# Groups of 8, 8, 8, 4, 4, 4 tiles in the routing of a retention + expert + SoLU kernel, parts of its first loads, and the order of two short stretches

## The chip, the cores and the metric

One Trainium2 chip, of which the kernel uses one core. The metric is device time in microseconds (us) of one execution. Engines by their short names: PE (TensorE, matmuls), DVE (VectorE), ACT (ScalarE), POOL (GpSimd), SP (SyncE, which issues most DMAs).

## What is computed

Three blocks in a row, on 8 batches of 576 positions (4608 tokens, 512 features), all in float32:

```python
# 1: retention attention, 8 heads of 64
scores = (q @ k.T) / 8
ret = scores * where(i >= j, gamma[h] ** (i - j), 0)   # a decay, no softmax
x = ret @ v                                            # heads side by side: 4608 x 512
# 2: one expert of eight for each token
expert_idx = argmax(x @ w_gate); gate_w = softmax(x @ w_gate)[expert_idx]
out[mask_e] = gate_w * (relu(x[mask_e] @ w1[e]) @ w2[e])
# 3: SoLU feed-forward
h = out @ w_in                       # 512 -> 1024
solu = h * softmax(h); ln = (solu - mean) / sqrt(var + 1e-6) * g_ln
return ln @ w_out                    # 1024 -> 512
```

## The kernel before, in words

Each engine runs its instructions in the order in which the program writes them; there is no scheduler behind it.

**Stage 1, attention and routing (0 to about 166 us).** 40 chunks, n = 0 to 39: five for each batch, four of 128 positions and one of 64. `load(n)` brings keys, queries, scaled keys and values (`kc`, 1 MB; rows Q, KT, KR, VR), from SP, seven chunks ahead; chunks 0 and 1 come in two halves, and behind the first half of chunk 0 stand the tables `kt_t` (key decay) and `dt_t` (decay between positions, 640 KB). `prep(n)` scales K and Q on POOL (`kc`, `qp`). `scores(n)` (L445) makes `ps` on PE and multiplies it by the decay on DVE (`pp`, L448); `ps` has two buffers, which one chunk fills, so the scores of one chunk wait for the `pp` of the one before. `chunk(n)` adds the state's part (L466: `po` from `qp` and the state `st`) and the chunk's own (L474), then updates the state's sums (L483, `pu`) and copies them to `st` on DVE. `scores(n + 1)` is written ahead of `chunk(n)`. Each 128 finished tokens go through `xtile` (L517: transposed, with the gate's logits beside it, `px`), and when a group of tiles is full, `route(g)` begins.

`route` is a generator: one-hots of the top expert (`oha`), ranks on PE (`pr`, L581 to L585), the gate weight, the scaled tokens `xo` (written to DRAM as `xd`), the index lists by two one-hot tables (`m`, L189 to L195) and a product on PE (`inverse`, `pm`, L203). `tick(budget)` takes steps of it after each chunk; a `yield "pe"` holds it until the next chunk. Groups up to the last but two hold twice ahead of the ranks and twice ahead of `inverse`. With group EARLY (3) the first expert is settled: `count` (L241), its list, and the gathers of its tokens on POOL (L368).

**Stage 2, experts (to about 633 us).** For each expert 8 hidden blocks twice (`ph`, L854: three products of split halves), `hh` and `hl` on ACT and DVE, then outputs (`py`, L869), copied by ACT to `yo` (two buffers) and written to `yd` by SP (L977, L979). Weights come by `raw` (L170) and are split in `wh` (ACT) and `wl` (DVE, L179). `plan` works beside the first expert, by steps written between the blocks (`step`): it finds where each token of the sorted list goes. It writes the lists to DRAM (`sd`, L287) and gathers 36 columns from there (`got`, L318, POOL).

**Stage 3, feed-forward (to the end).** Tiles are taken in pairs q. `prod(q, i)` makes pieces of the first matmul (hx, hy, hz, L1059); `b11`, `b12`, `b21`, `b22` sum two pieces into a tile `wof` and take its maximum on DVE (L1072); `smax` (L1088, L1091), `ssum`, `root`, `norm` make the softmax and the normalisation; `ltrans` transposes the tile on PE (`ptl`, L1142) and splits it; `proj` is the last matmul (`pf`, L1157); `split` halves the inputs of a later pair. For q = 0 the order is written out apart. A tile's `wof` has two buffers.

Of the kernel before, what the change touches and what calls it, by code (L numbers as in the profile page):

```python
# [9 lines left out]
F32 = mybir.dt.float32  # L10
# [26 lines left out]
GROUPS = [8, 8, 8, 6, 3, 3]  # L37
# [85 lines left out]
def kernel(ctx: ExitStack, tc, kvc, kq4, v4, wg, w12, win, wout, gln,  # L123
# [8 lines left out]
    sd = tc.dram_tile([P * NCOL, 1], I32, name="sd")  # L132
# [111 lines left out]
    def plan(pool, col, then):  # L244
# [42 lines left out]
        nc.sync.dma_start(sd.rearrange("(p c) o -> p (c o)", p=P), src)  # L287
        then(numi)
        yield
# [13 lines left out]
        V.tensor_tensor(out=ge, in0=ge, in1=bc(gap, 1, NTT), op=ALU.mult)  # L303
        yield
        V.tensor_reduce(out=off, in_=ge, axis=AX.X, op=ALU.add)
        yield
        ii = T("ii", 2, NTT, dt=I32)
        V.tensor_tensor(out=off, in0=off, in1=C("slot"), op=ALU.add)
        V.tensor_scalar(out=ii[:, 0], in0=off, scalar1=float(NCOL * P - 1), scalar2=None, op0=ALU.min)
        yield  # L310
        V.tensor_scalar(out=ii[:, 1], in0=ii[:, 0], scalar1=7, scalar2=None, op0=ALU.logical_shift_right)
        V.tensor_scalar(out=ii[:, 0], in0=ii[:, 0], scalar1=P - 1, scalar2=None, op0=ALU.bitwise_and)
        yield
        V.scalar_tensor_tensor(out=ii[:, 0], in0=ii[:, 0], scalar=float(NCOL), in1=ii[:, 1], op0=ALU.mult, op1=ALU.add)
        yield
# [28 lines left out]
        V.scalar_tensor_tensor(out=ii[:, 0], in0=tt[:, 1], scalar=2.0 ** 20, in1=tt[:, 0], op0=ALU.mult, op1=ALU.add)  # L344
        yield
        V.tensor_scalar(out=smod, in0=ii[:, 0], scalar1=P - 1, scalar2=None, op0=ALU.bitwise_and)
        V.tensor_scalar(out=sdiv, in0=ii[:, 0], scalar1=7, scalar2=None, op0=ALU.logical_shift_right)
        V.tensor_tensor(out=dst, in0=got, in1=big, op=ALU.add)
# [24 lines left out]
    with ExitStack() as ax:  # L373
# [21 lines left out]
        def load(n):  # L395
# [60 lines left out]
        def chunk(n, ready):  # L456
# [4 lines left out]
            old, new = st[(c + 1) % 2], st[c % 2]  # L461
            po = ps_o.tile([P, 2, NP, P], F32, name="po")[:, :, :2]
            if c > 0:
                for pr in range(NP):
                    for h2, r in enumerate(HALF):
                        nc.tensor.matmul(po[HALF[h2 ^ pr % 2], pr % 2, pr // 2, :cl], old[r, pr, :], qp[r, pr, :cl],  # L466
                                         start=(pr < 2), stop=False, skip_group_check=True)
            for pr in range(NP):
                for to, r_ in enumerate(HALF):
                    h2 = to ^ pr % 2  # L470
                    h, r = 2 * pr + h2, HALF[h2]
                    a, w = (kc[:, VR, h * D:h * D + D], pp[:, h2, pr, :]) if c < 4 else \
                        (kc[r, VR, pr * D:pr * D + D], pp[r, 0, pr, :cl])
# [887 lines left out]
```

## Time and profile before

| | us |
|---|---|
| three runs | 1055.81, 1056.70, 1058.21 (median 1056.7) |
| the profiled execution | 1054.61 |
| its span, first to last instruction | 1052.8 |
| PE busy in it | 1010.9 (96%) |
| DVE, ACT, POOL busy | 652.1, 450.4, 269.2 |
| mean granted clock of PE | 0.986 of 2.4 GHz |

The rows below are of that one execution. In a row of the timeline stand start, duration, engine, line, operation, the tiles written and read, their shape, a count (`x16`: sixteen alike in a run), and in brackets how long the engine was idle ahead of it and what ended the idle time. PEld is PE's weight load. A row SPq is SP's queue of issues; DMA transfers are named by the tile that they fill.

### The profile page before, as it was taken

The numbers are of one execution on the slowest core, as the hardware profiler recorded it, in microseconds if no ns is written. First come the engines' busy times: TensorE is split into PE (matmuls) and PEld (weight loads), VectorE is DVE, ScalarE is ACT, GpSimd is POOL, SyncE is SP. The second block draws the span as 40 slices with busy tenths as digits, with TensorE's granted clock in tenths as the row PEclk, the third lists the DMA queues.
The fourth block names the chain that finished last, engine by engine and source line by source line (L and its number), as shares of the span: only waits on it lengthen the run. The fifth ranks groups of instructions, "written<-read, shape, count | busy, mean of one in ns | idle before, by whom it ended". The sixth has DMA issues, their size and how long they took to land.

```text
span 1052.8 us, 20697 instructions
## 1 busy us (share of the span) xinstructions
PE 1010.9 (96%) x8108; PEld 918.7 (87%) x8108; DVE 652.1 (62%) x1646; ACT 450.4 (43%) x847; POOL 269.2 (26%) x290
## 2 busy tenths in 40 slices
PE   5999996999999999999999999799999999999997
PEld 5888885899999999999999998588888888888885
DVE  3466786543447787789963426666657666666652
ACT  1344344333333344444333426455554555545542
POOL 3626421177310202010100021232232232322211
PEclk9999997999999999999999999899999999999999
DMA  9877973255243534354542231111111111111001
GB/s 333 332 245 298 339 252 133 82 165 167 79 162 114 193 124 167 128 188 153 169 141 102 103 106 39 50 42 49 41 50 50 52 51 40 51 41 41 24 28 42
DMA packets 52614, 130.77 MB, mean 124 GB/s; under 512 B 7680, under 2 KB 22272, under 8 KB 48672
## 3 DMA queue, kind: packets, MB, share of 16 engines
q1 hardware_dynamic: 45312, 109.94, 30.3%
q0 software_dynamic: 7200, 19.46, 5.7%
q8 instruction: 66, 1.08, 0.4%
q14 instruction: 36, 0.29, 0.1%
HBM read 99.95 MB, written 29.42 MB: 123 GB/s over the span
## 4 chain that ended last, share of the span: by engine, by line
PE 76%; DVE 1%; issue 1%; ACT 1%; DMA 1%; POOLq 0%; POOL 0%; ACTq 0%
PE py L869 20%; PE ph L854 20%; PE pf L1157 17%; PE hx L1059 7%; PE hz L1059 4%; PE hy L1059 4%; PE ptl L1142 3%; PE px L837 1%; DMA x<-xd,src 0%; DVE wof L1099 0%; ACT raw L1102 0%; ACT wh L1144 0%; DMA out_dram<-o__11972,dst 0%; DMA out_dram<-o__12074,dst 0%; ACT raw L1091 0%
## 5 line engine op out<-in xcount | busy, mean ns | idle before, releaser
L869 PE MATMUL py<-hh,wh 128*128 128x344 f32 (+7 forms) x512 | 157.6, 308 | 0.0
L869 PE MATMUL py<-hl,wh 128*128 128x344 f32 (+7 forms) x512 | 154.7, 302 | 0.0
L869 PE MATMUL py<-hh,wl 128*128 128x344 f32 (+7 forms) x512 | 154.5, 302 | 0.0
L368 POOL DMA_INDIRECT x<-xd,src x42 | 42.5, 1012 | 284.2 <-PE px L837 222.8
L856 ACT ACTIVATE hh<-ph 128x344 fp32r<-128x344 f32 (+7 forms) x128 | 53.6, 424 | 109.1 <-PE ph L854 105.5
L179 DVE TENSOR_TENSOR wl<-raw,wh 128x1024 fp32r<-128x1024 f32 x64 | 78.5, 1227 | 33.0 <-ACT wh L178 32.8
L869 PEld LDWEIGHTS py<-hh,wh 128*128 128x128 f32 x512 | 96.4, 188 | 0.1
L869 PEld LDWEIGHTS py<-hh,wl 128*128 128x128 f32 x512 | 96.5, 188 | 0.0
L869 PEld LDWEIGHTS py<-hl,wh 128*128 128x128 f32 x512 | 96.2, 188 | 0.0
L854 PE MATMUL ph<-xh,wh 128*128 128x344 f32 (+7 forms) x512 | 94.0, 306 | 1.1 <-ACT xh L840 1.1
L854 PE MATMUL ph<-xl,wh 128*128 128x344 f32 (+7 forms) x512 | 94.0, 306 | 0.0
L854 PE MATMUL ph<-xh,wl 128*128 128x344 f32 (+7 forms) x512 | 94.0, 306 | 0.0
L857 DVE SCALAR_TENSOR_TENSOR hl<-ph,hh 128x344 fp32r<-128x344 f32 (+7 forms) x128 | 60.1, 471 | 52.2 <-ACT hh L856 52.1
L871 ACT COPY yo<-py 128x344 f32<-128x344 f32 (+7 forms) x64 | 26.5, 413 | 141.8 <-PE py L869 111.8
L1157 PE MATMUL pf<-wol,wh 128*128 128x512 f32 x288 | 80.5, 402 | 0.0
L854 PEld LDWEIGHTS ph<-xh,wh 128*128 128x128 f32 x512 | 79.0, 191 | 1.3 <-ACT xh L840 1.3
L854 PEld LDWEIGHTS ph<-xl,wh 128*128 128x128 f32 x512 | 79.0, 190 | 0.2 <-DVE xl L841 0.2
L854 PEld LDWEIGHTS ph<-xh,wl 128*128 128x128 f32 x512 | 79.0, 190 | 0.0
L1145 DVE TENSOR_TENSOR wl<-ptl,wh 128x512 fp32r<-128x512 f32 x72 | 49.5, 689 | 47.6 <-ACT wh L1144 47.6
L1157 PE MATMUL pf<-woh,wh 128*128 128x512 f32 x288 | 76.4, 406 | 1.5 <-ACT wh L1144 1.5
L1157 PE MATMUL pf<-woh,wl 128*128 128x512 f32 x288 | 71.8, 391 | 0.0
L178 ACT CAST wh<-raw 128x1024 fp32r<-128x1024 f32 x64 | 67.0, 1047 | 0.0
(605 smaller groups left out, 2120.5 us busy)
## 6 DMA issues: line engine op xcount, KB each, us to landing
raw<-in_w_dram SPq DMA_DIRECT2D x64, 512.0 KB, 3.5
kc<-in_kvc_dram SPq DMA_DIRECT2D x30, 1024.0 KB, 7.7
yg<-yd SPq DMA_DIRECT2D x72, 128.0 KB, 2.2
xd<-xo SPq DMA_DIRECT2D x3, 2048.0 KB, 8.8
f<-in_win_dram SPq DMA_DIRECT2D x16, 256.0 KB, 3.8
f<-in_wout_dram SPq DMA_DIRECT2D x16, 256.0 KB, 3.7
kc<-in_kvc_dram SPq DMA_DIRECT2D x4, 512.0 KB, 8.4
kc<-in_kq_dram SPq DMA_DIRECT2D x8, 256.0 KB, 7.7
```

The source lines that it names most:

```text
L178: nc.scalar.copy(wh, raw)
L179: V.tensor_tensor(out=wl, in0=raw, in1=wh.bitcast(F32), op=ALU.subtract)
L368: nc.gpsimd.indirect_dma_start(out=x[:w, i, :], out_offset=None, in_=xd[:rows, :], in_offset=bass.IndirectOffsetOnAxis(ap=src[:w, e * CT + ...
L854: nc.tensor.matmul(ph, w[:, w0 + kb * P:w0 + kb * P + P], xx[:, kb, cc], start=(n == 0), stop=(n == 3 * KD - 1))
L856: nc.scalar.activation(out=hh[:, cc], in_=ph, func=AF.Relu)
L857: V.scalar_tensor_tensor(out=hl[:, cc], in0=ph, scalar=0.0, in1=hh[:, cc].bitcast(F32), op0=ALU.max, op1=ALU.subtract)
L869: nc.tensor.matmul(p, w[:, ff], h[:, cc], start=(n == 0), stop=(n == 3 * NFB - 1))
L871: nc.scalar.copy(yo[:, cc], p)
L1059: nc.tensor.matmul(p, x[:, 2 * a + k], m[:, w, k], start=(first and k == 0 and i == 0), stop=(k == 1 and i == 2), skip_group_check=True)
L1142: nc.tensor.transpose(p[:, kb, :], u[:, f * P:f * P + P], ident)
L1145: V.tensor_tensor(out=ll[:, fs, :], in0=p, in1=lh[:, fs, :].bitcast(F32), op=ALU.subtract)
L1157: nc.tensor.matmul(pfs[t], a[:, f, :], w[f // 2][:, f % 2, :], start=(n == 0), stop=(n == m - 1))
```

## The change

It does four things.

At the start, the decay table comes as its first 1024 columns (512 KB) and, after chunk 3, the last 256. The second half of chunk 0 comes as values and then scaled keys, 256 KB each. The products of chunk 1 with the state and its state products are written ahead of the scores of chunk 2.

Groups are 8, 8, 8, 4, 4, 4 and not 8, 8, 8, 6, 3, 3; group 3 holds once and not twice; `tick` has larger budgets from chunk 31 on.

`plan` makes the lists on PE: it transposes the list table (48 x 128), writes eight lists of 6 x 128 one after the other at register offsets into one row in DRAM, reads that row back as 36 x 128 and transposes it again. The gathers go, and so do the index operations for them.

In the third stage, for q = 0, `b11(2)`, `ltrans(1, 1)`, `ltrans(2, 0)` and `prod(2, 3)` change places.

```diff
-GROUPS = [8, 8, 8, 6, 3, 3]
+GROUPS = [8, 8, 8, 4, 4, 4]
...
-    sd = tc.dram_tile([P * NCOL, 1], I32, name="sd")
+    sd = tc.dram_tile([1, NT + CT * P], F32, name="sd")
...
-        nc.sync.dma_start(sd.rearrange("(p c) o -> p (c o)", p=P), src)
         then(numi)
+        sf = T("sf", NCOL)
+        V.tensor_copy(sf[:, :CT], src[:, :CT])
+        V.tensor_copy(sf[:, CT:], f.rearrange("p i c -> p (i c)"))
+        row = pool.tile([NTT, P], F32, name="row")
+        V.memset(row, 0.0)
+        nc.sync.dma_start(sd[0, :NT].rearrange("(t p) -> t p", p=P), row)
+        for _ in range(5):
+            yield
+        pt = psum.tile([NCOL, P], F32, name="pst", tag="pr")
+        nc.tensor.transpose(pt, sf, ident)
+        lists = pool.tile([NCOL, P], F32, name="lists")
+        V.tensor_copy(lists, pt)
...
-        got = T("got", NTT, dt=I32)
-        for t in range(NTT):
-            nc.gpsimd.indirect_dma_start(
-                out=got[:, t:t + 1], out_offset=None, in_=sd[:, :],
-                in_offset=bass.IndirectOffsetOnAxis(ap=ii[:, 0, t:t + 1], axis=0))
+        for e in range(E):
+            nc.sync.dma_start(sd[0, bass.ds(at[e], CT * P)].rearrange("(c p) -> c p", p=P), lists[e * CT:(e + 1) * CT])
             yield
...
+        nc.sync.dma_start(row, sd[0, :NT].rearrange("(t p) -> t p", p=P))
...
+        pd = psum.tile([P, NTT], F32, name="psd", tag="pr")
+        nc.tensor.transpose(pd, row, ident[:NTT, :NTT])
+        V.tensor_tensor(out=dst, in0=pd, in1=big, op=ALU.add)
...
                 if n == 0:
+                    nc.sync.dma_start(dt_t[:, :H * P], dtab[:, :H * P])
+                    nc.sync.dma_start(kc[:, VR], kvc[b, c, :, VR * DM:(VR + 1) * DM])
                     nc.sync.dma_start(kt_t, ktab)
-                    nc.sync.dma_start(dt_t, dtab)
-                nc.sync.dma_start(kc[:, 2:], kvc[b, c, :, 2 * DM:].rearrange("p (a f) -> p a f", a=2))
+                    nc.sync.dma_start(kc[:, KR], kvc[b, c, :, KR * DM:(KR + 1) * DM])
+                else:
+                    nc.sync.dma_start(kc[:, 2:], kvc[b, c, :, 2 * DM:].rearrange("p (a f) -> p a f", a=2))
...
+            if n == 1:
+                upd()
+                scores(n + 1)
+                prep(n + 2)
...
-            tick(1.0)
+            tick(1.0 if n < NN - 9 else 1.5)
...
-            if g < len(GROUPS) - 2:
+            if g < EARLY:
                 yield "pe"
...
         qdma(2 * P, S - P)
+        nc.sync.dma_start(dt_t[:, H * P:], dtab[:, H * P:])
...
-            if n > 0:
+            if n > 1:
                 scores(n + 1)
...
-            tick(0.8 if n < NN - 3 else 2.0)
+            tick(0.8 if n < NN - 9 else 1.5 if n < NN - 3 else 2.0)
...
                     ssum(t + 2)
-                    b11(q + 2)
                     smax(t + 3)
...
                     prod(q + 2, 2)
+                    ltrans(t + 1, 1)
+                    b11(q + 2)
                     root(t + 3)
-                    ltrans(t + 1, 1)
+                    prod(q + 2, 3)
+                    split(q + 3, 1)
                     norm(t + 3)
-                    ltrans(t + 2, 0)
-                    split(q + 3, 1)
...
                 proj(t + 1, 0)
+                if q == 0:
+                    ltrans(t + 2, 0)
...
-                prod(q + 2, 3, 4)
+                prod(q + 2, *((3, 4) if q else (4,)))
```

`upd` is the state update that stood at the end of `chunk` before (the products into `pu` and the copy to `st`). The memset of `wgi` goes ahead of the first `prep`, and the cast of `tri` from chunk 0 to chunk 2.

The start on PE, before: the first rows of its program, from the scores of chunk 0 on (`x16` covers the scores of chunks 1 and 2).

```order
L445 MATMUL ps<-kc 128x128 x8
L474 MATMUL po<-pp,kc 64x128 x8
L483 MATMUL pu<-kc 64x64 x8
L445 MATMUL ps<-kc 128x128 x16
L466 MATMUL po<-qp,st_126 64x128 x8
L474 MATMUL po<-pp,kc 64x128 x8
L483 MATMUL pu<-kc 64x64 x8
L517 MATMUL px<-wgi,xts 64x136 x8
```

And with the change (L448 is `scores` now, L481 the state's part, L493 the chunk's own, L472 the state products):

```order
L448 MATMUL ps<-kc 128x128 x8
L493 MATMUL po<-pp,kc 64x128 x8
L472 MATMUL pu<-kc 64x64 x8
L448 MATMUL ps<-kc 128x128 x8
L481 MATMUL po<-qp,st_126 64x128 x8
L472 MATMUL pu<-kc 64x64 x8
L448 MATMUL ps<-kc 128x128 x8
L493 MATMUL po<-pp,kc 64x128 x8
L528 MATMUL px<-wgi,xts 64x136 x8
```

The scores of chunk 2 stood right behind those of chunk 1; now two pieces of chunk 1 stand between them.

The last chunks on DVE, before, from the decay products of chunk 38 (`pp`, L448) to those of chunk 39 (L450): the scaling and the index chain of group 3, of which three operations follow later.

```order
L448 TENSOR_TENSOR pp<-ps,dt_t 128x512 x2
L485 COPY st_126<-pu 128x256
L567 TENSOR_SCALAR xo<-xr,gt 128x512 x3
L598 TENSOR_SCALAR far<-rka 128x6
L599 SCALAR_TENSOR_TENSOR tm<-tm,rka 128x6
L602 SCALAR_TENSOR_TENSOR sl<-far,tm 128x6
L604 TENSOR_SCALAR smod<-sl 128x6
L605 TENSOR_SCALAR sdiv<-sl 128x6
L189 TENSOR_TENSOR m_2466<-cs,smod 128x768
L450 TENSOR_TENSOR pp<-ps,dt_t 128x4x64
```

With the change the same chain stands between the products of chunks 36 and 37 (`pp`, L451):

```order
L451 TENSOR_TENSOR pp<-ps,dt_t 128x512 x2
L474 COPY st_126<-pu 128x256
L578 TENSOR_SCALAR xo<-xr,gt 128x512 x2
...
L616 TENSOR_SCALAR sdiv<-sl 128x4
L189 TENSOR_TENSOR m_2345<-cs,smod 128x512
L192 TENSOR_TENSOR m_2346<-cs,sdiv 128x4x48
L194 TENSOR_SCALAR m_2346<-m_2346,cs 128x4x48
L195 TENSOR_TENSOR m_2346<-m_2346,cs 128x4x48
L179 TENSOR_TENSOR wl<-raw,wh 128x1024
L451 TENSOR_TENSOR pp<-ps,dt_t 128x512 x2
```

It is complete now ahead of the next products, and a weight split (`wl`) stands behind it.

The third stage on DVE, q = 0, before, from the first of `ssum` (L1104) to the second tile's sum (L1099):

```order
L1104 TENSOR_SCALAR rs__8333<-s__8236 128x1
L1105 RECIPROCAL rs__8333<-rs__8333 128x1
L1107 SCALAR_TENSOR_TENSOR r_8336<-rs__8333 128x1
L1072 ISA wof,hm<-hy,xs_8264 128x512
L1072 ISA hm 128x1
L1088 TENSOR_SCALAR nm<-hm 128x1
L1114 TENSOR_SCALAR v<-v,r_8336 128x1
L1099 ISA wof,nu<-raw,wof 128x1024
```

And with the change (L1085 would be `b11`, L1101 the negated maximum, L1112 the sum):

```order
L1117 TENSOR_SCALAR rs__8309<-s__8212 128x1
L1118 RECIPROCAL rs__8309<-rs__8309 128x1
L1120 SCALAR_TENSOR_TENSOR r_8312<-rs__8309 128x1
L1101 TENSOR_SCALAR nm<-hm 128x1
L1127 TENSOR_SCALAR v<-v,r_8312 128x1
L1112 ISA wof,nu<-raw,wof 128x1024
```

The two rows of `b11` are gone from here; they stand 12 rows further down, behind the splits of the transposed tile (`wl`).

## Rows read from the trace of the kernel before

**Rows 1.** Busy time by stretch: busy us and instructions of each engine, clock, DMA share, GB/s.

```profile
0.00:26.30 26.30, 15.54 (x220) 13.97 (x222) 8.75 (x18) 3.81 (x6) 9.02 (x13) 0.94 0.94 333
157.90:184.20 26.30, 16.17 (x231) 14.22 (x226) 17.75 (x76) 11.96 (x26) 3.21 (x3) 0.74 0.39 133
658.00:684.00 26.00, 18.57 (x83) 15.21 (x83) 17.67 (x48) 10.74 (x20) 5.56 (x8) 0.87 0.18 51
```

**Rows 2.** Timeline of the start, PE and POOL.

```profile
10.22 1.97 PE L474 MATMUL po<-pp,kc 128*64 128x128 f32 x16 [3.29 <-DMA kc<-in_kvc_dram]
...
16.92 1.04 POOL L421 TENSOR_TENSOR kc<-kc,kt_t 128x512 f32<-128x512 f32 x1 [1.89 <-DMA kc<-in_kvc_dram]
...
16.99 2.08 PE L445 MATMUL ps<-kc 64*128 64x128 f32 x16 [2.62 <-DVE wgi L689]
...
19.00 1.13 PE L466 MATMUL po<-qp,st 64*64 64x128 f32 x16
...
20.89 1.04 POOL L421 TENSOR_TENSOR kc<-kc,kt_t 128x512 f32<-128x512 f32 x1 [1.70 <-DMA kc<-in_kvc_dram]
...
21.10 0.63 PE L483 MATMUL pu<-kc 128*64 128x64 f32 x16
...
22.59 1.16 PE L445 MATMUL ps<-kc 64*128 64x128 f32 x16
```

**Rows 3.** Timeline of the end of stage 1, PE, then DVE.

```profile
150.72 1.75 PE L445 MATMUL ps<-kc 64*128 64x128 f32 x16 [0.91 <-DVE pp L448]
...
155.68 1.16 PE L445 MATMUL ps<-kc 64*128 64x128 f32 x16
...
159.79 0.62 PE L445 MATMUL ps<-kc 64*64 64x64 f32 x14
...
169.38 0.17 PE L581 MATMUL pr<-oha,tri 128*128 128x24 bf16 x1 [2.80 <-DVE oha L549]
...
173.13 0.42 PE L203 MATMUL pm<-m,m 128*128 128x96 bf16 x3 [3.51 <-DVE m L195]
...
177.90 1.94 PE L837 MATMUL px<-cs,x 128*128 128x128 f32 x8 [2.56 <-DMA x<-xd,src]
...
151.52 1.48 DVE L179 TENSOR_TENSOR wl<-raw,wh 128x1024 fp32r<-128x1024 f32 x1
152.92 1.28 DVE L448 TENSOR_TENSOR pp<-ps,dt_t 128x512 f32<-128x512 f32 x2
...
159.32 1.27 DVE L567 TENSOR_SCALAR xo<-xr,gt 128x512 f32<-128x512 f32 x3
...
163.60 0.46 DVE L195 TENSOR_TENSOR m<-m,cs 128x288 bf16<-128x288 bf16 x1
```

**Rows 4.** Timeline of the third stage's first pair, DVE, ACT and PE.

```profile
665.78 0.69 DVE L1072 CUSTOM_DVE_ANT_0 wof<-hy,xs 128x512 f32<-128x512 f32 x1 [1.41 <-PE ptl L1142]
...
666.70 1.15 ACT L1091 ACTIVATE raw<-wof,nm 128x1024 f32<-128x1024 f32 x1 [1.45 <-DVE nm L1088]
...
672.58 1.09 PE L1142 MATMUL ptl<-cs,wof 128*128 128x128 f32 x4 [6.83 <-DVE v L1114]
...
677.27 0.39 PE L1059 MATMUL hy<-wih,xh 128*128 128x512 f32 x1
...
678.64 0.39 PE L1059 MATMUL hx<-wih,xh 128*128 128x512 f32 x1
```

**Rows 5.** Timeline inside expert 0, PE and DVE.

```profile
210.36 0.79 PE L854 MATMUL ph<-xh,wh 128*128 128x344 f32 x4
...
210.84 0.51 DVE L857 SCALAR_TENSOR_TENSOR hl<-ph,hh 128x344 fp32r<-128x344 f32 x1
```

**Rows 6.** SP's waits from 200 to 300 us, and timeline of SP and ACT.

```profile
SPq L979 <- DMA yd<-yo: 9.1, 4, 3.4
...
220.13 1.09 SPq L170 DMA_DIRECT2D raw<-in_w_dram  x2
...
246.78 0.45 ACT L871 COPY yo<-py 128x344 f32<-128x344 f32 x1 [2.27 <-issue]
```

More of the change, by code (lines that the diff above doesn't have):

```diff
@@ L242, in count, with plan @@
         V.tensor_copy(cnt, pc)
-    def plan(pool, col, then):
+    def plan(pool, psum, col, at, then):
         T = lambda nm, *shape, dt=F32: pool.tile([P] + list(shape), dt, name=nm)
@@ L302, in plan @@
         yield
[L303 to L315, printed above, removed]
-        got = T("got", NTT, dt=I32)
-        for t in range(NTT):
-            nc.gpsimd.indirect_dma_start(
-                out=got[:, t:t + 1], out_offset=None, in_=sd[:, :],
-                in_offset=bass.IndirectOffsetOnAxis(ap=ii[:, 0, t:t + 1], axis=0))
+        ii = T("ii", NTT, dt=I32)
+        for e in range(E):
+            nc.sync.dma_start(sd[0, bass.ds(at[e], CT * P)].rearrange("(c p) -> c p", p=P), lists[e * CT:(e + 1) * CT])
             yield
@@ L460, in chunk, with upd @@
             pp = pt.pop(n)
[L461 to L473, printed above, removed]
-                    nc.tensor.matmul(po[r_, pr % 2, pr // 2, :cl], a, w, start=(c == 0 and pr < 2), stop=(pr >= 2),
-                                     skip_group_check=True)
-            if c < 4:
+            def upd():
                 if c == 0:
@@ L485, in chunk @@
                 V.tensor_copy(new, pu)
+            old, new = st[(c + 1) % 2], st[c % 2]
+            po = ps_o.tile([P, 2, NP, P], F32, name="po")[:, :, :2]
+            if c > 0:
+                for pr in range(NP):
+                    for h2, r in enumerate(HALF):
+                        nc.tensor.matmul(po[HALF[h2 ^ pr % 2], pr % 2, pr // 2, :cl], old[r, pr, :], qp[r, pr, :cl],
+                                         start=(pr < 2), stop=False, skip_group_check=True)
+            if n == 1:
+                upd()
+                scores(n + 1)
+                prep(n + 2)
+            for pr in range(NP):
+                for to, r_ in enumerate(HALF):
+                    h2 = to ^ pr % 2
+                    h, r = 2 * pr + h2, HALF[h2]
+                    a, w = (kc[:, VR, h * D:h * D + D], pp[:, h2, pr, :]) if c < 4 else \
+                        (kc[r, VR, pr * D:pr * D + D], pp[r, 0, pr, :cl])
+                    nc.tensor.matmul(po[r_, pr % 2, pr // 2, :cl], a, w, start=(c == 0 and pr < 2), stop=(pr >= 2),
+                                     skip_group_check=True)
+            if c < 4 and n != 1:
+                upd()
             g0 = b * S + o
@@ L608, in route @@
             yield "pe"
-            if g < len(GROUPS) - 2:
+            if g < EARLY:
                 yield "pe"
@@ L669 @@
         load(6)
+        V.memset(wgi[:, :, :P], 0.0)
+        V.memset(ones, 1.0)
         prep(0)
@@ L672 @@
         prep(1)
-        V.memset(ones, 1.0)
         nx = [0]
@@ L686 @@
             if n == 0:
-                V.memset(wgi[:, :, :P], 0.0)
                 for h2, r in enumerate(HALF):
@@ L690 @@
                     V.tensor_copy(wgi[r, 1:KD:2, HALF[1 - h2]], bc(ident[r, r], 1, KD // 2))
+            if n == 2:
                 V.tensor_copy(tri, C("tri"))
@@ L905, in others @@
             yield
-            yield from plan(sp, beg, settled)
+            yield from plan(sp, ps_r, beg, at, settled)
             sx.close()
```

14 lines of the change are left out of this document (7 added, 7 removed).

## Prediction

> **What bounds the kernel now.** I read the page's busy shares first: TensorE (PE) works 1010.9 of the 1052.8 us, so at most some 42 us can be had from any reordering, and only where PE stands still. So next the busy time by stretch: PE is full nearly everywhere but in three stretches of about 26 us [rows 1], which lose 10.8, 10.1 and 7.4 us: the start, the end of the attention stage, and the first pair of tiles of the third stage. In two of them the granted clock is down too (0.74 and 0.87 on average), so each idle there also makes matmuls behind it slow. Last I read in time order what each idle of PE waited for in these three, because that tells which wait ends last. The change touches all three, and one stretch where PE is full now.
>
> A time that differs from 1056.7 us by less than 0.2% (2.1 us) I count as no change. The sum is made against the profiled execution, 1054.6 us, which is 2.1 us under the median of the runs; that offset is added back at the end.
>
> **A. The start.** At 10.22 PE waits 3.29 us for the second half of chunk 0 [rows 2], which stands fourth in SP's queue behind the 640 KB decay table. Of the chain behind it everything to the scores of chunk 1 comes about 1 us earlier when that half goes in two parts and the last 128 KB of the table go later. But PE then stands before the scores of chunk 2, at 16.99. The row blames DVE, whose work ended long before; POOL starts on chunk 2 at 16.92 after waiting 1.89 us for its DMA, so it is the landing of chunk 2. In that landing only the 128 KB count that are no longer ahead of it: at 333 GB/s, the rate of the stretch [rows 1], 0.39 us. What is gained besides is the work that is moved into the wait: the products of chunk 1 with the state, 1.13 us at 19.00, and its state products, 0.63 us at 21.10 [rows 2]. Both can run before 16.6, since they need nothing of chunk 2 and the scaled query tile is ready by then. Sum 0.39 + 1.13 + 0.63 = 2.15. What is late next: the scores of chunk 3, at 22.59 now, cannot start before chunk 3 has landed, 20.89 - 0.39 = 20.5, so at most 2.1 are kept. **I take 2.0 us.** Low end 1.0, if the two pieces don't both fit in the wait; high end 2.9: the scores took 2.08 us at 16.99 and 1.16 us at 22.59 for the same 16 matmuls, and that 0.92 comes back if the shorter idle leaves the clock up. Two more issues on SP cost nothing as long as POOL waits for landings, which it does at 16.92 and 20.89. The memset that moves ahead lies in DVE's idle time.
>
> **B. Groups 8, 8, 8, 4, 4, 4.** Now three waits stand at the end of the stage [rows 3]: 2.80 us (the one-hots of group 4), 3.51 us (its index chain on DVE), 2.56 us (the gathered tiles, which come late because the lists come late); ahead of them a 0.91 us wait of scores for DVE. Together 9.78. With smaller groups, one hold less and larger budgets, group 3 ends two chunks earlier and group 4 is routed among the last chunks; the lists and the gathers come with it, so 2.80, 3.51 and 2.56 go. New waits take their place, because the same DVE work now stands between the decay products that scores wait for. PE needs 4.1 us for a chunk that waits for nothing (155.68 to 159.79). Between two products DVE now has: state copy 0.42, two scalings and nine index operations, some 3.0 us (from 159.32 to 164.06 it took 4.74, of which 0.84 was other work, for six tiles and three scalings; four tiles and two scalings are a little less), a weight split of 1.48, the products themselves 1.28: 6.2, so PE waits about 2.1 us. One chunk earlier the one-hots and another 1.48 us split stand there beside a short chunk: about 1.85 us by the same working. The count then waits for three small DVE operations, about 0.95. And the index chain of group 4 takes 3.75 us now from ranks (169.38) to its products (173.13), with four tiles and a second scaling some 4.3, against 1.5 us of chunk 39 that PE has beside it: 2.8 us. Sum of new waits 7.7, gain 9.78 - 7.7 = 2.1. **I take 2.1 us.** Low end -1, if each new wait lowers the clock behind it and a wait costs a microsecond more; high end 5, if the two waits before scores are covered.
>
> **C. First pair of the third stage.** PE stands idle 6.83 us before 672.58 [rows 4]. The row names DVE, and the chain behind it begins with one DVE operation: the sum and maximum at 665.78, which waits 1.41 us for PE's transposes because it writes the tile that they read. Everything behind it on DVE waits too, first the negated maximum, so that ACT's exponential starts at 666.70; it could have started 1.4 us earlier. With that operation put behind the transposes' consumers, the chain starts 1.41 us sooner. Also six products (677.27 to 678.64, 1.37 us) and not the next tile's transposes now stand in the idle time; these transposes had been held by DVE and go behind the projection. 1.41 + 1.37 = 2.78. **I take 2.8 us.** Low end 2.0, if the operation that is moved makes the products late (DVE reaches it some 5 us later, and ACT still has gaps there); high end 4.6, if the idle, then near 3.3 us, leaves the clock up.
>
> **D. The plan of the lists.** Removed: 36 gathers on POOL. They lie beside experts where PE is full, so nothing is gained. Added on PE: two transposes. The first stands right ahead of the products that start at 210.36 [rows 5]. Its operand is made by DVE, which is then behind: it does the split at 210.84 until 211.35, then three conversions of about 0.15 us each. So PE waits about 1.4 us and spends 0.2 on it. **I take -1.6 us.** Ends: -0.3 if DVE runs ahead there, -4 if the clock falls. The second comes seven hidden blocks into expert 1, after the row was read back: covered. Added on SP: a chain of nine writes, each of which waits until the one before it has landed, ahead of the output writes of expert 0. At a spacing as it is now that is covered too; it is the first rival.
>
> Sum: 2.0 + 2.1 + 2.8 - 1.6 = 5.3. 1054.6 - 5.3 = 1049.3, and 2.1 more to the median: **1051.4 us**.
>
> **Rivals.**
>
> *1. The chain of list writes makes expert 0 late (slower).* SP gets to it at about 219.6, shortly before the weight load that it issues at 220.13 now [rows 6]. Behind the nine writes stand two weight loads and the output writes; the write that frees ACT's output buffer lands about 12.2 spacings on. ACT's copy at 246.78 needs that buffer, and PE has PSUM tiles to go on until about 253. So nothing is lost below (253 - 219.6) / 12.2 = 2.74 us a link, and 1.22 us for each 0.1 above it. Now a second output write waits 9.1 / 4 = 2.28 us for the first, and with 0.35 to issue a link is 2.6; a third of that moves 344 KB, the lists 3 KB. So it speaks for no loss that a link is near 2; against, that the longest wait was 3.4 us, and that two links have a 512 KB weight load ahead of them. At 3.4 us a link it costs 8.1 us: 1059.5. It passes the mark for slower, 1058.8, at 3.35. The Trainium skill (DMA: Bandwidth & Descriptors, "Latency and other measured facts") has HBM access at 0.2 us on average and 2 us at high load. By that rule a loaded link would be some 1.8 us longer, 4.4 us, and the time about 1072, an estimate; of the four waits here only the longest, 3.4 us, hints at it. Chance 0.11, of which 0.07 slower.
>
> *2. The regrouping gives nothing.* DVE's work of two groups comes into the last chunks, and if it can't be hidden the waits are only spread: B is -1, the time 1054.5. For it: 0.91 us are lost to DVE already at 150.72. Against: the 8.87 us that go are seen and named. Chance 0.13, half of it within 0.2%.
>
> *3. The clock stays up.* In the three stretches idles of 2.6 to 6.8 us are followed by matmuls at 1.2 GHz; with shorter idles A, B and C may be 2.9, 3.5 and 4.6: 2.9 + 3.5 + 4.6 - 1.6 = 9.4, so 1047.3. Against: 2.0 to 3.3 us of idle remain in each. The Trainium skill (TensorE: Matmul & The Clock Gate, "What's actually happening") says that the low level is the default and that activity releases it. By that rule denser work in these stretches would hold 2.4 GHz; that the means there are 0.94, 0.74 and 0.87 [rows 1] agrees, but no row shows how short an idle has to be. Chance 0.14.
>
> **How the numbers follow.** The forecast itself, all four parts inside their bounds, 0.62. Faster by over 0.2% (under 1054.6): 0.62 + 0.14 + 0.07 = 0.83. Within: 0.06 + 0.04 = 0.10. Slower (over 1058.8): 0.07. The range: below, rival 3 with D at its small end and a little of B, 1045.5; above, rival 2 and a part of D's clock loss, 1056.5; rival 1 in full is left outside.
>
> **What would show it.** A: PE's scores of chunk 3 near 20.5, the two moved pieces before 16.6. B: the products of the gathered tiles some 4 us earlier than 177.90 with A; waits of 1 to 3 us for DVE in the last chunks. C: the idle before the projection at about 3.3 us and not 6.83. D: a wait of about 1.4 us before a transpose inside expert 0, and SP's list writes at 2 to 2.6 us spacing. I'd be wrong if PE shows idle time near 250 (rival 1), or if the waits of DVE before scores sum to over 6 us.

## Result, and the profile after

| | before | changed |
|---|---|---|
| median of 6 runs, us | 1056.35 | 1046.94 |
| lowest and highest | 1054.63, 1058.21 | 1045.0, 1050.27 |
| the profiled execution | 1054.61 | 1045.0 |
| its span | 1052.8 | 1043.2 |

The ratio is 0.9911, 95% interval 0.9894 to 0.9928: 9.4 us faster (7.6 to 11.2). A second comparison at the end of the study gave 0.9903 (0.9880 to 0.9925). The forecast was 1051.4 us: the right way, inside its range, and 4.5 us short.

In two of the four sessions of the experiments (e5 to e8, one execution each, and e9 to e11) the kernel before took 1096 to 1102 us and not 1056 in every run, so whole times are compared within a session only; e9 asks why.

Busy time in the three stretches, changed kernel (columns as in [rows 1]):

```profile
0.00:26.30 26.30, 19.20 (x302) 16.90 (x304) 8.72 (x20) 5.13 (x10) 9.55 (x13) 1.00 0.96 339
157.90:184.20 26.30, 21.82 (x255) 19.64 (x252) 18.94 (x76) 12.34 (x29) 4.96 (x6) 0.94 0.36 119
658.00:684.00 26.00, 22.92 (x100) 18.39 (x99) 17.83 (x52) 13.73 (x25) 8.71 (x9) 0.87 0.13 41
```

PE is busy 3.7, 5.7 and 4.4 us longer in them than before, and the clock of the first two is 1.00 and 0.94, where it was 0.94 and 0.74 [rows 1]. In the third it stays at 0.87.

The start in the changed kernel, timeline, POOL and PE:

```profile
8.09 1.03 POOL L424 TENSOR_TENSOR kc<-kc,kt_t 128x512 f32<-128x512 f32 x1 [7.65 <-DMA kc<-in_kvc_dram]
...
13.45 0.67 PE L481 MATMUL po<-qp,st 64*64 64x128 f32 x16 [0.20 <-POOL qp L430]
...
14.04 0.69 PE L472 MATMUL pu<-kc 128*64 128x64 f32 x16
...
15.04 1.07 POOL L424 TENSOR_TENSOR kc<-kc,kt_t 128x512 f32<-128x512 f32 x1 [1.64 <-DMA kc<-in_kvc_dram]
...
15.10 1.16 PE L448 MATMUL ps<-kc 64*128 64x128 f32 x16 [0.37 <-DVE wgi L701]
...
18.94 1.04 POOL L424 TENSOR_TENSOR kc<-kc,kt_t 128x512 f32<-128x512 f32 x1 [1.60 <-DMA kc<-in_kvc_dram]
...
19.01 1.16 PE L448 MATMUL ps<-kc 64*128 64x128 f32 x16 [0.79 <-DMA kc<-in_kvc_dram]
```

The two moved pieces (13.45 and 14.04) end at 14.7, ahead of the scores of chunk 2, as they should. But chunk 2 lands (POOL begins on it) at 15.04 and not 16.5, chunk 3 at 18.94 and not 20.5, and the scores of chunk 2 take 1.16 us and not 2.08. The scores of chunk 3 begin at 19.01, 3.6 us earlier than before, after waiting 0.79 us for that landing.

The end of stage 1, timeline, PE:

```profile
144.38 1.75 PE L448 MATMUL ps<-kc 64*128 64x128 f32 x16 [0.97 <-DVE pp L451]
146.06 1.67 PE L493 MATMUL po<-pp,kc 128*64 128x128 f32 x16
...
153.87 1.75 PE L448 MATMUL ps<-kc 64*128 64x128 f32 x16 [0.56 <-DVE pp L451]
...
159.57 0.17 PE L241 MATMUL pcnt<-run,ones 128*128 128x8 bf16 x1 [0.66 <-DVE run L633]
...
167.62 0.34 PE L203 MATMUL pm<-m,m 128*128 128x96 bf16 x4 [2.44 <-DVE m L195]
...
168.97 1.65 PE L850 MATMUL px<-cs,x 128*128 128x128 f32 x12
...
172.22 0.90 PE L867 MATMUL ph<-xh,wh 128*128 128x344 f32 x4 [0.80 <-ACT xh L853]
...
174.02 1.35 PE L867 MATMUL ph<-xh,wl 128*128 128x344 f32 x4
```

The waits before scores are 0.97 and 0.56 us, the count waits 0.66, the index products 2.44. The gathered tiles (168.97) no longer wait, and their twelve products take 1.65 us. Before, they came as four and eight, with waits of 0.67 and 2.56 us ahead of them, and took 1.11 and 1.94 us [rows 3]. Two more rows of PE in the trace of before, around those of [rows 3]:

```profile
174.23 1.11 PE L837 MATMUL px<-cs,x 128*128 128x128 f32 x4 [0.67 <-DMA x<-xd,src]
...
180.51 1.51 PE L854 MATMUL ph<-xh,wh 128*128 128x344 f32 x4 [0.59 <-ACT xh L840]
```

The hidden products begin at 172.22 and not at 180.51. That is 8.3 us, of which 3.3 come from the start.

The third stage's first pair, timeline, ACT and PE:

```profile
651.41 1.19 PE L1170 MATMUL pf<-woh,wh 128*128 128x512 f32 x4 [0.59 <-ACT wh L1157]
...
657.93 1.13 ACT L1104 ACTIVATE raw<-wof,nm 128x1024 f32<-128x1024 f32 x1
...
662.98 3.78 PE L1170 MATMUL pf<-woh,wh 128*128 128x512 f32 x8 [3.08 <-ACT wh L1157]
...
666.56 1.91 PE L1170 MATMUL pf<-wol,wh 128*128 128x512 f32 x4
...
672.03 1.18 PE L1170 MATMUL pf<-wol,wh 128*128 128x512 f32 x4
```

and the projections in the trace of before, ahead of the idle, behind it and one further on, PE:

```profile
658.64 1.20 PE L1157 MATMUL pf<-woh,wh 128*128 128x512 f32 x4 [0.60 <-ACT wh L1144]
...
673.32 3.19 PE L1157 MATMUL pf<-woh,wh 128*128 128x512 f32 x8
...
676.34 1.09 PE L1157 MATMUL pf<-wol,wh 128*128 128x512 f32 x4
...
681.71 1.18 PE L1157 MATMUL pf<-wol,wh 128*128 128x512 f32 x4
```

ACT's exponential no longer waits for DVE. PE stands idle 3.08 us and not 6.83, 3.75 less. But the twelve products behind the idle (662.98 and 666.56) take 5.5 us, where they took 4.1 before (673.32 and 676.34); with the clock up they take 3.1 (e10). From the projection ahead of the idle to the second part of the next one, the pair takes 20.6 us (651.41 to 672.03), before it 23.1 (658.64 to 681.71): 2.4 us. So 1.3 of the 3.75 us went to the clock.

The plan, timeline, PE:

```profile
202.53 0.29 PE L297 MATMUL pst<-cs,sf 128*48 128x128 f32 x1 [1.14 <-DVE sf L290]
```

and SP:

```profile
210.39 0.41 SPq L293 DMA_DIRECT2D sd<-row  x1
...
225.51 0.37 SPq L990 DMA_DIRECT2D yd<-yo  x1
```

PE waits 1.14 us ahead of the transpose; with it 1.4 us are lost. SP issues the first of the nine writes at 210.39 and the first output write at 225.51: 15.1 us for nine links, 1.68 us each. PE has no idle time behind it.

So the 9.6 us by which the span is shorter are, read off between equal matmuls in both traces: start 3.3 (as it stands ahead of the scores of chunk 35), end of stage 1 5.8, plan -1.9, first pair 2.4. Of the 5.8, 1.1 lie behind the second set of gathered tiles: 1.5 because the clock fell there before and does not now, less a wait that is 0.4 longer.

### The profile page after: what moved, and what is told of

The parts are those of the page before. It is cut to its first block, busy times and chain, and to the rows that moved or that the text cites. A ratio compares the mean times of both kernels' runs of the same rounds, so it can differ in the third digit from the quotient of the medians.

```text
span 1043.2 us, 20687 instructions
## 1 busy us (share of the span) xinstructions
PE 1012.7 (97%) x8110; PEld 918.3 (88%) x8110; DVE 648.1 (62%) x1642; ACT 449.5 (43%) x847; POOL 231.1 (22%) x254
## 4 chain that ended last, share of the span: by engine, by line
PE 75%; DVE 3%; issue 2%; ACT 1%; DMA 1%; POOLq 0%; POOL 0%; ACTq 0%
PE py L882 21%; PE ph L867 19%; PE pf L1170 16%; PE hx L1072 7%; PE hz L1072 4%; PE hy L1072 4%; PE ptl L1155 3%; PE px L850 2%; DVE wof L1112 1%; DMA x<-xd,src 0%; ACT raw L1115 0%; DVE wof L1085 0%; DMA out_dram<-o__11948,dst 0%; DMA out_dram<-o__12050,dst 0%; ACT raw L1104 0%
## 5 line engine op out<-in xcount | busy, mean ns | idle before, releaser
L178 ACT CAST wh<-raw 128x1024 fp32r<-128x1024 f32 x64 | 67.0, 1047 | 0.0
```

The costliest lines, as they stand in the source:

```text
L178: nc.scalar.copy(wh, raw)
```

## Experiments

### e1 to e3: each part alone

e1 is part A, e2 part B, e3 part C of the diff above, each put on the kernel before.

> Part A alone on the kernel before (loads in parts, chunk 1's state work ahead of the scores of chunk 2, the small moves on DVE). Theory from the trace after: the start is worth what the scores of chunk 3 show there, 22.59 - 19.01 = 3.6 us, of which 3.3 are left at chunk 35; so 1056.4 - 3.4 = 1053.0 us, with the scores of chunk 3 near 19.0 and of chunk 2 near 15.1 at full clock. Rival, the prediction's price: 2.0 us, so 1054.4, the rest of the 3.3 being work that the new groups took out of the stage.

> Part B alone on the kernel before (groups 8, 8, 8, 4, 4, 4, one hold less, larger budgets). Theory: the end of the stage is worth 5.8 us, because the waits that it puts before scores are only 1 us and 0.6 us, and because the clock falls once and not twice; so 1050.6 us, first products of expert 0 about 5.1 us earlier than 180.51. Rival, the prediction's price: 2.1 us, so 1054.3, with waits of about 2 us before the scores of chunks 36 and 38.

> Part C alone on the kernel before (order of the third stage's first pair). Theory: 2.4 us, as the trace after has it between two products on either side; so 1054.0 us. Rival: the prediction's 2.8, with the idle time before the projection at 3.1 us in both cases; a gain under 1.5 would say that the start of the pair depends on parts A and B.

| | ratio to before | 95% interval | gain, us | read off the trace |
|---|---|---|---|---|
| e1, start | 0.9977 | 0.9965 to 0.9989 | 2.4 (1.2 to 3.7) | scores of chunk 3 at 19.02, chunk 2 lands at 15.02 |
| e2, groups | 0.9964 | 0.9943 to 0.9985 | 3.8 (1.6 to 6.0) | 3.2 from chunk 33 to the hidden products |
| e3, pair | 0.9982 | 0.9968 to 0.9995 | 1.9 (0.5 to 3.4) | 19.6 us for the pair, 23.1 before: 3.5 |

The start repeats to 0.02 us in its trace (3.57), so it is the loads and the order, not the groups. The interval of its measured gain takes in both the forecast's 2.0 and the 3.4 of the theory. In its profile 3.4 us are left at chunk 39 (156.43 against 159.79), and 1.4 are lost at the third stage's first pair, where the twelve products took 5.5 us and not 4.1. What is won at chunk 3 is not always kept either, see e12. The groups alone are worth less than the 5.8 read off the changed kernel, and the interval takes in both that and the prediction's 2.1. Its trace shows why: a further wait ahead of the scores of chunk 34, which the changed kernel's profile has not.

```profile
141.94 0.68 PE L445 MATMUL ps<-kc 64*64 64x64 f32 x16 [1.33 <-DVE pp L448]
...
150.46 1.75 PE L445 MATMUL ps<-kc 64*128 64x128 f32 x16 [0.97 <-DVE pp L448]
...
159.89 1.75 PE L445 MATMUL ps<-kc 64*128 64x128 f32 x16 [0.50 <-DVE pp L448]
...
173.65 0.34 PE L203 MATMUL pm<-m,m 128*128 128x96 bf16 x4 [2.44 <-DVE m L195]
```

From the scores of chunk 33 to those of chunk 39 PE takes 29.3 us here, 27.7 in the changed kernel, 24.2 before; from there to the hidden products 12.5, 12.6 and 20.7. So in these two profiles the groups lose 3.5 to 5.1 us ahead of chunk 39 and win 8.2 behind it. What is lost is waits for DVE, scores at half clock behind them (1.75 us and not 1.16), and products that now stand there and not later. The same stretch takes 27.5 us in the profile of e4, 28.5 in that of e12, and 34.0 in that of e10, so a single profile gives its size only roughly.

### e4: the changed kernel with the old plan

Edit: `plan`, the two lines that call it, and `sd` as before.

> The changed kernel with the plan of before (lists to DRAM as a table, 36 gathers on POOL, no transposes, no chain of writes). Theory: the transpose's wait of 1.1 us, the transpose itself and some 0.5 us behind it come back, so about 1.9 us under the changed kernel, 1045.0. Rival: the gathers cost something now that the stage before is shorter (POOL is late with the tokens of expert 1), then 1047 or more.

Measured: 1047.12 us, ratio 0.9918 (0.9898 to 0.9937), against 0.9911 for the whole change: not told apart. In the trace the price is there: between two equal hidden blocks the changed kernel takes 3.30 us with the transpose (199.33 to 202.63), e4 1.90 (204.25 to 206.15), so 1.40. Up to the first output products it is 0.1 more, and 0.4 between the first products of expert 1 and the third stage, where the second transpose stands (255.91); the trace doesn't tie the 0.4 to it. The theory's 1045.0 was missed, and the rival's "1047 or more" came, but not for its reason: PE is full beside the gathers in e4's profile. What that profile lost lies ahead of them: the clock fell behind the second set of gathered tiles, which waited 2.17 us and not 1.55, and that took 1.5 us. So -1.9 is the price by the traces, and it is smaller than what differs between executions in other places.

### e5 to e7: what brings the chunks in earlier

e5 is the loads alone, with the order of chunk 1 as before. In e6 and e7 part A is whole but for these lines:

```diff
 e6 (table cut, half of chunk 0 in one piece), against part A:
                     nc.sync.dma_start(dt_t[:, :H * P], dtab[:, :H * P])
-                    nc.sync.dma_start(kc[:, VR], kvc[b, c, :, VR * DM:(VR + 1) * DM])
                     nc.sync.dma_start(kt_t, ktab)
-                    nc.sync.dma_start(kc[:, KR], kvc[b, c, :, KR * DM:(KR + 1) * DM])
-                else:
-                    nc.sync.dma_start(kc[:, 2:], kvc[b, c, :, 2 * DM:].rearrange("p (a f) -> p a f", a=2))
+                nc.sync.dma_start(kc[:, 2:], kvc[b, c, :, 2 * DM:].rearrange("p (a f) -> p a f", a=2))
...
 e7 (key table first), against part A:
+                    nc.sync.dma_start(kt_t, ktab)
                     nc.sync.dma_start(dt_t[:, :H * P], dtab[:, :H * P])
                     nc.sync.dma_start(kc[:, VR], kvc[b, c, :, VR * DM:(VR + 1) * DM])
-                    nc.sync.dma_start(kt_t, ktab)
                     nc.sync.dma_start(kc[:, KR], kvc[b, c, :, KR * DM:(KR + 1) * DM])
```

> On the kernel before, the loads in parts alone, with the order of chunk 1's work as before. Theory: the landings make most of the start's gain; chunk 2 lands at 15.0 to 15.4 (POOL's scaling of it, 16.5 to 16.9 in the three profiles with the old loads), and the scores of chunk 3 begin at about 20 to 20.7, since 1.8 us of chunk 1's work still stand behind the scores of chunk 2. Rival, the prediction's working: only the 128 KB count, chunk 2 lands near 16.5 and the scores of chunk 3 begin near 22.2.

> Part A, but the second half of chunk 0 comes in one piece of 512 KB behind the key table (the decay table is still cut). If the split into 256 KB pieces makes the early landings, chunk 2 lands near 16.5 again and the scores of chunk 3 begin near 20.5. If the order of the small key table (16 KB in rows of 128 B) or the cut of the decay table makes them, chunk 2 lands at 15.0 to 15.4 and the scores of chunk 3 begin at 19.0 to 19.4.

> Part A, but the small key table (16 KB) ahead of the decay table, as before. If its rows of 128 B ahead of the large transfers make the low rate that the kernel before shows from 3 to 4.6 us (127 to 213 GB/s), chunk 2 lands some 0.8 to 1.2 us later than in the changed kernel, near 16, and the scores of chunk 3 begin near 20. If not, landings are those of the changed kernel, 15.0 and 19.0.

POOL's scaling of chunk 2, which begins when it has landed, in e6:

```profile
15.24 1.04 POOL L421 TENSOR_TENSOR kc<-kc,kt_t 128x512 f32<-128x512 f32 x1 [1.68 <-DMA kc<-in_kvc_dram]
```

and in e7:

```profile
17.30 1.04 POOL L424 TENSOR_TENSOR kc<-kc,kt_t 128x512 f32<-128x512 f32 x1 [1.68 <-DMA kc<-in_kvc_dram]
```

SP's issue of chunk 2's load, in e6:

```profile
6.53 1.18 SPq L408 DMA_DIRECT2D kc<-in_kvc_dram  x1
```

and in e7:

```profile
6.95 3.02 SPq L411 DMA_DIRECT2D kc<-in_kvc_dram  x1
```

| | order in SP's queue | SP's issue of chunk 2's load ends | chunk 2 lands | scores of chunk 3 |
|---|---|---|---|---|
| before | key table, table 640 KB, half | 9.76 | 16.92 | 22.59 |
| e7 | key table, table 512 KB, two quarters | 9.97 | 17.30 | 21.38 |
| e5 | table 512 KB, quarter, key table, quarter; old order of work | 8.04 | 15.40 | 21.16 |
| e6 | table 512 KB, key table, half | 7.71 | 15.24 | 19.21 |
| changed | table 512 KB, quarter, key table, quarter | 7.54 | 15.04 | 19.01 |

e5's landing came as its theory said, its scores of chunk 3 some 0.5 us later; in e7 both are over 1 us later than either value that was expected. The split does nothing that is seen (e6). What matters is where the 16 KB key table stands: issued ahead of the large table, it makes chunk 2 land 1.9 to 2.3 us later than behind it. The rows of SP show where that comes from. In the kernel before and in e7 SP needs 3.0 to 3.5 us to issue chunk 2's load, in the three others 0.3 to 1.2, and in all five chunk 2 lands 7.2 to 7.5 us behind the end of that issue. Why the issue is held when the key table comes first is not shown. The table has 128 rows of 128 B; whether its short rows matter or only its place was not tried. With the key table first, the 128 KB that are cut off the large table bring nothing (17.30 in e7, 16.92 before).

The order of work brings 2.1 us with the new loads (21.16 in e5, 19.01 in the changed kernel) and 1.2 with the key table first (22.59 before, 21.38 in e7), so the start's gain can't be parted into a share for each.

The Trainium skill (DMA: Bandwidth & Descriptors, "Why small descriptors are slow (HBM only)") gives a small fixed overhead for each packet, 27% at 256 B. By that rule 16 KB would hardly be seen; the runs show 2 us for the place of this table in the queue, and they decide.

### e8: the list writes twice

```diff
         for e in range(E):
-            nc.sync.dma_start(sd[0, bass.ds(at[e], CT * P)]...
+            for _ in range(2):
+                nc.sync.dma_start(sd[0, bass.ds(at[e], CT * P)]...
```

> The changed kernel with each of the eight list writes made twice, one after the other, so 17 links in the chain and not 9. At the 1.7 us a link of the changed kernel (210.39 to 225.51 for nine) that puts the output writes of expert 0 some 13.6 us later. By the working of the first rival PE has a reserve up to about 246 for the write that frees ACT's buffer, which would then land near 247 to 249: PE idles 1 to 3 us or not at all. If the reserve is smaller than worked out, PE shows idle time of over 5 us between 230 and 255 and the time is 1050 or more.

Timeline, SP:

```profile
214.66 0.41 SPq L293 DMA_DIRECT2D sd<-row  x1
...
240.01 0.37 SPq L991 DMA_DIRECT2D yd<-yo  x1
```

ACT:

```profile
244.72 0.45 ACT L885 COPY yo<-py 128x344 f32<-128x344 f32 x1 [9.92 <-DMA yd<-yo]
```

PE:

```profile
252.82 1.41 PE L868 MATMUL ph<-xh,wh 128*128 128x328 f32 x4 [3.62 <-ACT xh L854]
...
266.66 0.25 PE L347 MATMUL psd<-cs,row 36*128 36x36 f32 x1 [1.24 <-DMA row<-sd]
```

17 links (a link is one write, issued when the one before it has landed) take 25.4 us, 1.49 each. ACT's copy waits 9.92 us for the output write, PE then 3.62, and 1.24 for the row that is read back. So the chain of the first rival is real, and it ends where it was placed. PE ran dry at 249.2; e8 is 4.0 us behind the changed kernel there (the outputs of expert 0 begin at 214.31 and at 210.29), so that is 245.2 in the changed kernel's time, and the reserve was put at about 246. The cost, 3.6 us, is over the 1 to 3 that were expected. The chain was 10.2 us longer and cost 3.6, so with nine links some 6.6 us are in hand.

### e9: the gathers put back

36 gathers of one 4-byte element a partition, which nothing uses, behind the list writes of the changed kernel:

```diff
+        got = T("got", NTT)
+        for t in range(NTT):
+            nc.gpsimd.indirect_dma_start(
+                out=got[:, t:t + 1], out_offset=None, in_=xd.rearrange("n (d o) -> (n d) o", o=1),
+                in_offset=bass.IndirectOffsetOnAxis(ap=src[:, t:t + 1], axis=0))
+            yield
```

> The changed kernel with 36 gathers on POOL put back as dead work behind the list writes (one 4-byte element a partition, as many and as large as those of the old plan; nothing uses them). In the trace of the loads alone, on a chip where the kernel before took 1096 us, every engine waits for its next instruction while the old plan's gathers run, 219.8 to some 247 us, and the changed plan ran there in 1056 with the list writes doubled. If the gathers are what starves the engines, this kernel takes 30 to 45 us more than the changed kernel on such a chip and the same within 2 us on a chip where the kernel before takes 1056. If it is another part of the old plan, it stays with the changed kernel on either chip.

Measured: 1090.58 us, beside 1099.52 for the kernel before and 1053.15 for e10, which has the changed plan, in the same session. Where it goes, by stretch, in e9 (270 to 300 us, the second run of gathers):

```profile
210.60:240.00 29.40, 20.75 (x109) 18.00 (x109) 5.96 (x13) 4.42 (x10) 19.48 (x19) 0.83 0.35 102
...
270.00:300.00 30.00, 13.23 (x51) 10.31 (x51) 2.63 (x4) 2.94 (x6) 17.43 (x19) 0.63 0.07 18
```

the same in e10:

```profile
210.60:240.00 29.40, 28.25 (x184) 27.92 (x183) 12.92 (x31) 9.57 (x16) 9.09 (x9) 1.00 0.41 127
...
270.00:300.00 30.00, 30.00 (x205) 29.97 (x204) 20.79 (x52) 11.30 (x22) 1.58 (x2) 1.00 0.42 137
```

and PE's waits in e9 (columns: total, times, longest):

```profile
PE ph L873 <- issue: 16.7, 15, 2.4
...
PE py L888 <- issue: 4.3, 7, 1.7
```

The gathers come in two runs, 13 from 219.1 to 235.9 us and 23 from 264.5 to 292.9, one each 1.25 us. In e9 PE works 13.2 of the 30 us around the second run, ACT 2.9 and DVE 2.6; PE waits for nothing that the profile shows (a wait named "issue"), up to 2.4 us ahead of one matmul. In e10, without the gathers, PE is full. e5 to e7, which have the old plan, show the same from 219.8 us on. The waits outlast the gathers by some 4 us (in e5 the last gather ends at 245.7, the waits at 249.7).

The three gathers of the first expert's tokens, which every version keeps, show it on a small scale. In e10, PE:

```profile
171.11 0.46 PE L481 MATMUL po<-qp,st 64*64 64x64 f32 x16 [1.37 <-issue]
```

From the count to the first hidden products, where they run, the new groups take 15.4 to 16.7 us in the profiles of e8 to e11, and 12.6 to 14.0 in those of the changed kernel, e2, e4 and e12.

So in such a session the gathers hold up every engine's instructions, at 35 to 37 us in all (1090.6 - 1053.2, of which up to 2.6 can be e10's filling), and the kernel before carries that cost: e9 is 8.9 us under it, about what the whole change brings in the first comparison. In the other sessions the same gathers stood beside a PE that was full. What differs between the sessions is not settled: the gathers take 0.94 us each in both, and the DMA engines are nearly idle while it happens (28 GB/s and less between 225 and 245 us of e5). The record gives the chip of e1 to e4 and that of e5 to e8 the same number, so that number does not part them.

### e10 and e11: matmuls into the idle time

e10 puts 12 useless matmuls (128x512) ahead of the first pair's projection, into the buffer that it starts anew; e11 also 16 small ones ahead of the index products of group 4.

```diff
                     prod(q + 2, 3)
+                    fill(t + 1, q + 2, 12)
...
+        for _ in range(fill):
+            nc.tensor.matmul(pm, ident, cs[:, :2 * NCOL].rearrange("p (a c) -> p a c", a=2), start=True, stop=True)
```

> The changed kernel with 12 useless matmuls (128x512, into the buffer that the projection starts anew) in PE's idle time ahead of the third stage's first projection. If the low clock behind the idle time is what it costs besides (12 matmuls of the projection took 5.7 us there, 3.0 at full clock), the projection runs at full clock and the pair ends 2.0 to 3.0 us earlier, with the granted clock of 658 to 684 us near 1.00 and not 0.87. Rival: what stands behind the projection waits for ACT and DVE anyway; then the clock rises and the next products start no earlier, 0 to 1 us.

> As the kernel with filled pair, and 16 useless small matmuls ahead of the index products of group 4 too, in PE's 2.4 us wait for DVE. Theory: the gathered tiles' and first hidden products then run at full clock, 1.5 to 2 us earlier on top; in sum 4 to 5 us under the changed kernel. Rival: the first hidden products wait for ACT and DVE (0.8 us now), and the clock falls behind that wait all the same: no more than with the pair alone.

e10, timeline, PE (12 filling matmuls, then the projection):

```profile
669.27 2.90 PE L1177 MATMUL pf<-wih,xh 128*128 128x512 f32 x12
672.51 2.17 PE L1170 MATMUL pf<-woh,wh 128*128 128x512 f32 x8 [0.34 <-ACT wh L1157]
674.52 1.08 PE L1170 MATMUL pf<-wol,wh 128*128 128x512 f32 x4
...
678.97 1.18 PE L1170 MATMUL pf<-wol,wh 128*128 128x512 f32 x4
```

The projection takes 3.1 us and not 5.5, and the pair 18.0 us (660.93 to 678.97) and not 20.6: 2.6 us, and the granted clock of 658 to 684 us is 1.00. The rival falls. But e4's profile has 18.0 without any filling (654.43 to 672.46), e3 and e12 19.6: the clock falls in some executions behind the same 3.1 us of idle and comes back sooner in others, so the filling takes away a chance, not a fixed cost. In all, the new order without filling took 18.0 to 20.8 us in six profiles, the old one 23.1 to 24.4 in six.

e11's ratio is 0.9531 (0.9506 to 0.9557), e10's 0.9588 (0.9536 to 0.9639). Of that difference the filling at the index products is not the cause: e11 is 4.2 us ahead of e10 at the count already, 161.66 against 165.88, before any filling, because its chunks waited less for DVE. From the count to the first hidden products e10 takes 16.0 us and e11 15.9. So that filling gained 0.1 us, as the rival had it, but not for the rival's reason. In e11, PE:

```profile
169.28 3.81 PE L203 MATMUL pm<-cs 128*128 128x96 f32 x32
```

The filling was longer than the idle that it was put into (2.89 us in e10): the index products begin 11.27 us behind the count and not 10.59. The clock did stay up behind it. The twelve products of the gathered tiles take 1.65 us and not 2.31, and from the index products to the hidden products it is 4.60 us and not 5.43. A shorter filling was not tried.

### e12: the changed kernel again

> The changed kernel unaltered, once more beside the kernel before, to have its time on a chip where the kernel before takes about 1098 us. Theory: without the gathers the engines are not starved there, 1052 to 1058 us, a ratio near 0.96 and not 0.99; the kernel with the pair filled (1053.2) then gains little or up to 3 us on it, the one with both filled (1047.8) 4 to 9. Rival: the fills are what made those two fast, and the changed kernel takes 1085 us or more there. On a chip where the kernel before takes 1056, about 1047 again.

The session was one in which the kernel before takes 1056.97 us: 1047.97, ratio 0.9903 (0.9880 to 0.9925), runs from 1043.3 to 1050.6. So the changed kernel's own time in the other kind of session was not measured; 1053 (e10) and 1056 (e8) are the nearest. Its profiled execution, 1050.6, is one of the long ones, and shows what is not kept of the start, PE's timeline:

```profile
86.93 1.75 PE L448 MATMUL ps<-kc 64*128 64x128 f32 x16 [1.96 <-DVE pp L451]
...
90.82 1.92 PE L528 MATMUL px<-wgi,xts 128*64 128x136 f32 x16
```

The scores of chunk 21 wait 1.96 us for DVE, 0.93 in the first profile, and 3.9 us further on sixteen products take 1.92 us and not 1.10. At chunk 22 it is 2.6 us behind the first profile, counted from chunk 4, and e4's profile 2.7; the first 0.8 (e12) and 0.5 (e4) of it were lost by chunk 7. Whether DVE's work of the first group falls before or behind these scores decides it; which early delay tips it was not tried; both profiles have PE idle at chunk 5 for nothing that the profile shows, 0.46 and 0.18 us.

No version was shown to beat the changed kernel: e11 took 1047.79 us in a session where e10 took 1053.15, but the changed kernel has no time there.

## Why the prediction was right, and where it was short

**What bounds the kernel: right.** What was won lies in the three stretches of [rows 1] and, 1.1 us of it, right behind the second; from 210.6 to 632 us PE was full before, and from 225 to 626 us it is full now.

**A, 2.0 forecast, 3.6 at chunk 3 and 2.4 (1.2 to 3.7) alone.** The order of work did what was said. The step that failed is "in that landing only the 128 KB count that are no longer ahead of it": the key table was moved too, and was not costed because it has only 16 KB. Its place is worth 2 us (e7), so chunk 3 landed at 18.94, where 20.5 had been the ceiling. The 128 KB by themselves, put at 0.39, can't be seen: with the key table first chunk 2 lands no earlier than before. The 0.92 us that were the high end came back as well, since the scores of chunk 2 ran at 2.4 GHz, but they hardly count: the scores of chunk 3 then waited 0.79 us for their chunk, so some 0.1 of the 0.92 is kept.

**B, 2.1 forecast, 3.8 (1.6 to 6.0) alone.** What is lost ahead of chunk 39 was near in sum: 4.9 forecast (1.85, 2.1 and 0.95), or 4.0 less the old wait of 0.91 that goes, and 3.5 to 5.1 found. That is partly luck, for it is made up otherwise: the waits before scores are 0.5 to 1.0 and not 1 to 3 us, and the rest lies in scores of 1.75 us, a chunk at half clock (146.06), in e2 a wait at chunk 34, and products that moved there. The index chain, 2.8, was 2.44. What was mis-sized is the end: 8.87 - 2.8 = 6.1 us were taken for what is behind chunk 39, and 8.2 came. The wait of 0.67 us for the first gathered tile went too and was left out of the sum, and the twelve products, which ran at half clock behind the old waits, take 1.65 and not 3.05 us. The last of them begin 8.9 us earlier than 177.90, where "some 4" was the sign.

**C, 2.8 forecast, 1.9 (0.5 to 3.4) alone, 2.4 by the two profiles.** The mechanism is right, the size partly luck. "Near 3.3 us" of idle does not follow from the sum: 6.83 - 2.78 is 4.05. The idle fell by 3.75, to 3.08: besides the two terms of the sum, which came as 1.5 and 1.4, the projection no longer stands behind the transposes that had waited for DVE (0.8), which the sum left out; and the slower clock of the twelve products took 1.3 back. By the clock the pair's gain lies anywhere from 2.3 to 6.4 us between the six profiles of either order.

**D, -1.6 forecast.** The wait was 1.14 us and not 1.4, with the transpose 1.4; 0.5 more are lost further on, most of it in the stretch of the second transpose, which I took as covered. The gathers "lie beside experts where PE is full, so nothing is gained": true in the sessions like that of the first comparison, and wrong by 35 to 37 us in others (e9). Nothing in the trace of before shows it.

**The rivals.** The chain of writes (1) has the mechanism and the place, and a link of 1.49 to 1.68 us, so no loss. The Trainium skill (DMA: Bandwidth & Descriptors, "Anatomy of one DMA — SWDGE (gpsimd) path") puts the fixed cost of a DMA that POOL issues at about 2.0 us. The writes here are of 3 KB, but for a first one of 18 KB, and SP issues them; a link took less, and the 4.4 us of the prediction were not seen. That the regrouping gives nothing (2) fell. The clock that stays up (3) came true in B, at the twelve products (1.4 us) and behind the second gathered tiles (1.5), hardly counted in A, and went the other way in C by 1.3. I had its price and gave it one chance in seven as a whole; it belonged into each term as an expectation.

**The sum.** Against the two profiles the forecast lacked 4.3 us: A 1.3, B 3.7, C -0.4, D -0.3. So the end of B is most of it, and the place of the key table the rest. That 1046.94 us stands next to the 1047.3 of rival 3 is luck: its terms were 2.9, 3.5, 4.6 and -1.6, and 3.3, 5.8, 2.4 and -1.9 came. The range held, with 1.4 us to spare at its lower end.

## What to carry to other kernels

Where PE's idle time shrinks to 1 to 3 us, price the matmuls behind it at both clocks and take a value between: some 3 us came from there here, and executions of one kernel differ by as much. A transfer's cost is not its bytes alone: try small tables at another place in the queue, behind what the first work needs, and read when the queue could issue the next load besides when that load landed. Work that an idle engine does beside a full one can still hold up the others' instructions; a comparison in one session doesn't show it.

## What the runs showed that I had not expected

- With a load of 16 KB issued ahead of one of 512 KB and not behind it, SP gets the load of chunk 2 out 1.9 to 2.4 us later (9.97 against 7.54 to 8.04), and it lands 1.9 to 2.3 us later (17.30 against 15.04 to 15.40).
- In some sessions 36 gathers of 4-byte elements from POOL, one each 1.25 us, leave PE 13.2 us of work in 30, with ACT and DVE held as well; in others the same gathers cost nothing that is seen.
- Nine writes to DRAM that wait for one another take 1.68 us each, 17 of them 1.49.
- The same idle of 3.1 us is followed by twelve matmuls in 5.5, 4.6 or 3.1 us in profiles of kernels that are alike there (changed kernel, e12, e4).
